# Two f tiles at a time through a two-layer network behind block attention, on one core

## The chip, the core and the metric

The kernel runs on one core of a Trainium2 chip. The engines of the core appear in the profile as PE (TensorE, matrix products, with PEld for its weight loads), DVE (VectorE), ACT (ScalarE), POOL (GpSimd) and SP (SyncE, which issues the DMAs here). The metric is the device time of one execution in microseconds (us); the number given for a kernel is the median of several runs. Times inside an execution come from one profiled execution, counted from its first instruction.

## The reference

Attention with a local window of 16 positions and, beside it, one summary key and value for each block of 32 positions; then a two-layer network with squared ReLU. B = 4 batches, H = 8 heads, S = 768 positions, D = 64; the network has 512 inputs, 2048 hidden units and 512 outputs.

```python
k_sum = k.reshape(B, H, nb, 32, D).max(axis=3)
v_sum = v.reshape(B, H, nb, 32, D).mean(axis=3)
scores_l = scale * q @ k.T          # kept where |i - j| < 16
scores_s = scale * q @ k_sum.T + log(32)
a = softmax(concat(scores_l, scores_s))
x = a @ concat(v, v_sum)            # heads side by side: 3072 tokens x 512
h = maximum(x @ w_in, 0)
out = (h * h) @ w_out
```

## The kernel before

**Tiling.** The 3072 tokens are 24 attention tiles g of 128 tokens, six (t = 0 to 5) for each batch b. Two tiles make a column block c (12 of them, CT = 256 tokens) for the network. The hidden units are 16 f tiles of 128 (NF). One f tile of one c is the unit of the network, here called a slot.

**The network.** Values are split in a high and a low part, so that each product is three matmuls: high by high, high by low, low by high. `ffn1(c, f)` (L306, matmuls at L311) is 12 matmuls of 256 columns from `xh` and `xl` into one tile `ph`. Then `squares(ph)` (L339): `relu` on ACT (L320), `high_square` on ACT (L327, gives `gh`), `square` on DVE (L332, in place in `ph`) and `low_square` on DVE (L336, gives `gl` and is the last to read `ph`). `ffn2` (L345, matmuls at L352) is 6 matmuls of 512 columns from `gh` and `gl` into the two tiles `o_ps[c]`, which gather over the 16 f tiles. `evict` (L358) copies each of the two `o_ps` tiles to `ob` on ACT (L105) and stores it; where an earlier part was parked (c = 0 and 1), it adds on DVE instead (L362).

**Buffers.** `ph` comes from a pool with three buffers (`ps_h`), `o_ps` from one with two, scores `s_ps` and attention outputs `x_ps` from one buffer each. `gh` and `gl` have three buffers each. `e_sb`, `ksum` and `vsum` exist once; `q_sb`, `k_sb`, `v_sb` and `pT` twice, by g even or odd.

**Order.** The whole program is issued in an order written out by hand: each engine takes its own instructions in that order. First comes the list START (all of attention tiles 0 to 5, the scores of tile 6, the rounding of the weights, the network of c = 0 and 1 up to f tile unit 29). Then `softmax(6, 0, 5)`, and the loop over c = 2 to 11 and f = 0 to 15, which calls `slot` (L384): `ffn1` of this f; `follow`, that is `ffn2` of two slots ago (BEHIND = 2, with both evictions after the last f of a c); the list `side`; `squares`; the list `last`. So PE has ffn1(f), ffn2(f-2), ffn1(f+1), ffn2(f-1) and so on.

**A tile's steps.** `steps(g)` (L396) spreads the attention of one tile over 11 slots; a new tile begins every 8 slots. Step 0: `place_k` (DVE, L151, only for t = 0 and 1 of a later batch, puts the block maxima into `k_sb`), at its end the scores (PE, L218) and the loads of q and k for tile g+2 (SP). Steps 1 to 3: `softmax` of 2, 3 and 3 heads, each head being one masked minimum on DVE (L231) and one exponential on ACT (L239). Steps 3 and 4: `inverse` (DVE, L248 and L249) and `norm` (POOL, L254) of each half. Steps 5 to 7: `turn`, 12 transposes on DVE (L267), four in each; step 6 also `place_v` (DVE and POOL). Step 9: `outputs` (PE, L280) and the load of v for tile g+2. Step 10: `split_x` (ACT L294, DVE L297). In tiles t = 3 and 4 of a batch the next batch's k and v are loaded pair by pair and reduced on DVE (`sum_k` L140, `sum_v` L145 and L148), two of the four pairs in each tile.

Of the kernel before, what the change touches and what calls it, by code (L numbers as in the profile page):

```python
# [12 lines left out]
F32R = mybir.dt.float32r  # L13
# [7 lines left out]
B, H, S, D = 4, 8, 768, 64  # L21
# [3 lines left out]
P = 128  # L25
NT = S // P
NPAIR = H // 2
TPC = 2
CT = TPC * P
NF = DF // P  # L30
NC4 = DM // P
SPARE = 1
BEHIND = 2
NK = 96 + NB
MASKED = -1.0e9

# [33 lines left out]
def attn_ffn_kernel(ctx: ExitStack, tc: tile.TileContext, q, k, kt, v, vt, v0, w, masks, ident, mean, out):  # L70
    nc = tc.nc
# [4 lines left out]
    work = ctx.enter_context(tc.tile_pool(name="work", bufs=2))  # L76
# [37 lines left out]
    def load_qk(g):  # L114
        load_q(g)
        load_k(g)

    def load_v(g):
        nc.sync.dma_start(out=v_sb[g % 2][0:96], in_=v[g // NT, g % NT])
# [13 lines left out]
    def load_kv(b, p):  # L133
        kv[b, p] = r = room(F32, "kv")
        nc.sync.dma_start(out=r[:, 0:S], in_=kt[b, p])
        if b:
            nc.sync.dma_start(out=r[:, S : 2 * S], in_=vt[b, p])

    def sum_k(b, p):
        nc.vector.tensor_reduce(  # L140
            out=ksum[:, p], in_=kv[b, p][:, 0:S].rearrange("a (n j) -> a n j", j=BLOCK), op=ALU.max, axis=AX.X
        )

    def sum_v(b, p):
        nc.vector.tensor_reduce(  # L145
            out=vsum[:, p, 0:NB], in_=kv[b, p][:, S : 2 * S].rearrange("a (n j) -> a n j", j=BLOCK), op=ALU.add, axis=AX.X
        )
        nc.vector.tensor_scalar_mul(vsum[:, p, 0:NB], vsum[:, p, 0:NB], 1.0 / BLOCK)  # L148

    def place_k(g):  # L150
        nc.vector.tensor_copy(out=k_sb[g % 2][:, 4], in_=ksum.unsqueeze(1).to_broadcast([P, 2, NPAIR, NB]))  # L151

    def place_v(g):
        dst = v_sb[g % 2][96:128]
        if g % 2 == 0:
            for a in range(4):
                nc.vector.transpose(
                    out=dst[:, 0, :].rearrange("a (p c) -> a p c", c=128)[:, :, a * 32 : a * 32 + 32],
                    in_=vsum[a * 32 : a * 32 + 32],
                )  # L160
        else:
            nc.gpsimd.tensor_copy(out=dst[:, 0, :], in_=v_sb[0][96:128, 0, :])
        nc.gpsimd.tensor_copy(out=dst[:, 1, :], in_=v_sb[0][96:128, 0, :])
# [46 lines left out]
    def scores(g, p0, p1):  # L210


        if g not in s_ps:
            s_ps[g] = ps_s.tile([P, 2, NPAIR, P], F32, name="s_ps")
        for p in range(p0, p1):
            for r, s in ((0, 0), (1, 1), (0, 1), (1, 0)):
                rs, ss = slice(r * 64, r * 64 + 64), slice(s * 64, s * 64 + 64)
                nc.tensor.matmul(  # L218
                    s_ps[g][ss, r, p, 0:NK], lhsT=q_sb[g % 2][rs, s, p, :], rhs=k_sb[g % 2][rs, :, s, p, :],
                    start=True, stop=True,  # L220
                )
# [19 lines left out]
    def softmax(g, h0, h1):  # L241

        for h in range(h0, h1):
            mask_max(g, h)
            exponentials(h)

    def inverse(half):
        nc.vector.tensor_scalar_add(sm[half], sm[half], 1.0e-9)  # L248
        nc.vector.reciprocal(sm[half], sm[half])  # L249
        del nmx[half]  # L250

    def norm(half, eng):
        e = e_sb[:, half * 4 : half * 4 + 4, 0:NK]
        eng.tensor_mul(out=e, in0=e, in1=sm[half].unsqueeze(2).to_broadcast([P, 4, NK]))  # L254
# [8 lines left out]
    def turn(g, n0, n1):  # L263

        blocks = [(i, j) for i in range(4) for j in ((0, 1, 3) if i % 2 == 0 else (1, 2, 3))]
        for i, j in blocks[n0:n1]:
            nc.vector.transpose(  # L267
                out=pT[g % 2][j * 32 : j * 32 + 32, :, i * 32 : i * 32 + 32],
                in_=e_sb[i * 32 : i * 32 + 32, :, j * 32 : j * 32 + 32],
            )  # L270
# [3 lines left out]
    def outputs(g):  # L274
        x_ps[g] = xp = ps_x.tile([P, NPAIR, P], F32, name="x_ps")

        for s in range(2):
            for h in range(H):
                o = (h % 2) * 64
                nc.tensor.matmul(  # L280
                    xp[o : o + 64, h // 2, s * 64 : s * 64 + 64],
                    lhsT=v_sb[g % 2][:, s, h * 64 : h * 64 + 64],
                    rhs=pT[g % 2][:, h, s * 64 : s * 64 + 64],
                    start=True, stop=True,
                )
# [13 lines left out]
    def split_x(g):  # L299
        high_x(g)  # L300
        low_x(g)
# [4 lines left out]
    def ffn1(c, f):  # L306
        ph = ps_h.tile([P, 4, P], F32, name="ph").rearrange("p a b -> p (a b)")[:, 0:CT]
        n = 0
        for cc in range(NC4):
            for w, x in ((0, xh), (1, xh), (0, xl)):  # L310
                nc.tensor.matmul(  # L311
                    ph, lhsT=w_sb[f][:, w, cc * P : (cc + 1) * P], rhs=x[c][:, cc, :], start=(n == 0), stop=(n == 3 * NC4 - 1)
                )
                n += 1
        return ph
# [7 lines left out]
        return r  # L323

    def high_square(r):
        gh = work.tile([P, CT], F32R, name="gh", tag="gh", bufs=3)
        nc.scalar.activation(gh, r, AF.Square)  # L327
        return gh

# [2 lines left out]
        nc.vector.tensor_mul(out=ph, in0=ph, in1=r)  # L332

    def low_square(ph, gh):
        gl = work.tile([P, CT], F32R, name="gl", tag="gl", bufs=3)
        nc.vector.tensor_sub(out=gl, in0=ph, in1=gh.bitcast(F32))  # L336
        return gl

    def squares(ph):  # L339
        r = relu(ph, nc.scalar)  # L340
        gh = high_square(r)
        square(ph, r)
        return gh, low_square(ph, gh)
# [30 lines left out]
    n_g = B * NT  # L374
    n_c = n_g // TPC
    behind = []
# [7 lines left out]
    def slot(c, f, side, last):  # L384


        ph = ffn1(c, f)
        if len(behind) == BEHIND:
            follow(*behind.pop(0))
        for do in side:  # L390
            do()
        behind.append((c, f, *squares(ph), f == 0, f == NF - 1))
        for do in last:
            do()

    def steps(g):  # L396


        b, t = divmod(g, NT)
        side, last = [[] for _ in range(11)], [[] for _ in range(11)]  # L400
        if b and t < 2:
            side[0].append(lambda: place_k(g))
            side[6].append(lambda: place_v(g))
        last[0].append(lambda: scores(g, 0, NPAIR))
        if g + 2 < n_g:
            last[0].append(lambda: load_qk(g + 2))
        side[1].append(lambda: softmax(g, 0, 2))
        side[2].append(lambda: softmax(g, 2, 5))
        side[3] += [lambda: inverse(0), lambda: norm(0, nc.gpsimd), lambda: softmax(g, 5, 8)]
        side[4] += [lambda: inverse(1), lambda: norm(1, nc.gpsimd)]  # L410
        for n in range(3):
            side[5 + n].append(lambda n=n: turn(g, 4 * n, 4 * n + 4))
        last[9].append(lambda: outputs(g))
        if g + 2 < n_g:
            last[9].append(lambda: load_v(g + 2))
        side[10].append(lambda: split_x(g))
        if b and t in (3, 4) and b + 1 < B:
            p = 2 * (t - 3)
            last[0].append(lambda: load_kv(b + 1, p))
            side[4] += [lambda: sum_k(b + 1, p), lambda: sum_v(b + 1, p)]  # L420
            last[4].append(lambda: load_kv(b + 1, p + 1))
            side[8] += [lambda: sum_k(b + 1, p + 1), lambda: sum_v(b + 1, p + 1)]
        return side, last


# [87 lines left out]
    with tc.manual_schedule(engines=None):  # L513
        for token in START.split():
            what, i, j, eng = re.fullmatch(r"(L:[a-z]+|F[12]|[A-Z]+)\.?(\d*)\.?(\d*)([avp]?)", token).groups()
            i, j = int(i or 0), int(j or 0)
            if what.startswith("L:"):
                load(what[2:], i)
            else:
                begin(what, i, j, engines.get(eng))  # L520
        tiles = {g: steps(g) for g in range(6, n_g)}

        def at(side, last, g, step):

            if g in tiles and 0 <= step < 11:
                side += tiles[g][0][step]
                last += tiles[g][1][step]

        load_qk(8)
        softmax(6, 0, 5)  # L530
        behind += [(*units[i][:2], *g_of[i], False, i == 31) for i in (30, 31)]
        for c in range(2, n_c):
            for f in range(NF):
                side, last = [], []
                at(side, last, 2 * c + 2, f + 3)
                at(side, last, 2 * c + 3, f - 5)
                at(side, last, 2 * c + 4, f - 13)
                slot(c, f, side, last)
        for p in behind:
            follow(*p)  # L540
# [67 lines left out]
```

## Time and profile before

| what | us |
|---|---|
| median of 3 runs | 644.5 (644.11 to 645.98) |
| the profiled execution | 646.57 |
| its span, first to last instruction | 644.8 |
| PE busy in the span | 609.8 (95%) |
| DVE busy | 403.3 (63%) |
| ACT busy | 300.4 (47%) |
| POOL busy | 108.8 (17%) |

The profiled execution's own time is 1.8 us above its span. The regular loop over slots takes from 149.7 us to the end. The busy time of PE is the time covered by its matmuls, which overlap one another: a matmul of 256 columns stands in the profile with a mean of 282 ns, but in the loop one starts about every 0.115 us. Rows of the timeline give the start, the duration, the engine, the line and the tiles written and read; in brackets stands the idle time before an instruction with what ended it.

### The profile page before, as it was taken

How to read it: one execution, taken by the hardware profiler on the slowest of the kernel's cores; microseconds unless marked ns; L12 is line 12 of the kernel's file. 1: busy time of each engine (PE TensorE's matmuls, PEld its weight loads, DVE VectorE, ACT ScalarE, POOL GpSimd, SP SyncE). 2: the span in 40 equal slices, each digit the busy share in tenths (PEclk: the TensorE clock that was granted, in tenths of full speed). 3: DMA queues.
4: the chain of work that ended last, by engine and by line, in shares of the span. 5: the costliest groups of instructions: out<-in, count | busy, mean ns of one | idle time of the engine just before them, and what ended most of it. 6: DMA issues, size and time to landing. Idle time of an engine off the chain costs nothing.

```text
span 644.8 us, 13041 instructions
## 1 busy us (share of the span) xinstructions
PE 609.8 (95%) x5052; PEld 536.3 (83%) x5052; DVE 403.3 (63%) x1223; ACT 300.4 (47%) x854; POOL 108.8 (17%) x85
## 2 busy tenths in 40 slices
PE   1678999999999999999999999999999999999997
PEld 0267988898888888898898898898888888898996
DVE  4678787656674686774774676874765665654232
ACT  2788866724335335345344344444344443443322
POOL 4465563501011011011011010010010010110000
PEclk9979999999999999999999999999999999999999
DMA  9999517004202314302102233301122020000000
GB/s 350 380 344 405 147 33 255 2 34 140 66 1 100 113 52 151 112 1 89 52 25 67 86 111 116 121 29 66 37 63 67 34 67 25 34 2 1 34 1 33
DMA packets 20429, 61.92 MB, mean 96 GB/s; under 512 B 2832, under 2 KB 2960, under 8 KB 18320
## 3 DMA queue, kind: packets, MB, share of 16 engines
q1 hardware_dynamic: 20368, 61.10, 27.6%
q8 instruction: 39, 0.64, 0.4%
q14 instruction: 22, 0.18, 0.1%
HBM read 54.80 MB, written 6.29 MB: 95 GB/s over the span
## 4 chain that ended last, share of the span: by engine, by line
PE 92%; DVE 3%; DMA 2%; ACT 1%; issue 1%; POOL 0%; SPq 0%; DVEq 0%; POOLq 0%; ACTq 0%
PE ph L311 42%; PE o_ps L352 40%; PE x_ps L280 4%; PE s_ps L218 4%; PE ph L260 1%; DMA k_sb<-in_k 1%; PE o_ps L126 1%; DMA w_raw<-in_w 1%; DVE pT L267 1%; DVE ksum L140 1%; ACT e_sb L239 0%; DVE k_sb L151 0%; ACT w_raw L189 0%; POOL e_sb L254 0%; ACT w_raw L185 0%
## 5 line engine op out<-in xcount | busy, mean ns | idle before, releaser
L311 PE MATMUL ph<-xh,w_sb 128*128 128x256 f32 x1536 | 280.4, 282 | 1.5 <-DVE gl L336 0.9
L311 PEld LDWEIGHTS ph<-xh,w_sb 128*128 128x128 f32 x1536 | 243.6, 188 | 18.8 <-issue 3.0
L352 PE MATMUL o_ps<-w_sb,gh 128*128 128x512 f32 x768 | 239.6, 393 | 0.0
L311 PE MATMUL ph<-xl,w_sb 128*128 128x256 f32 x768 | 213.9, 278 | 0.2 <-DVE xl L297 0.2
L332 DVE TENSOR_TENSOR ph<-ph,r 128x256 f32<-128x256 f32 x192 | 82.7, 431 | 125.0 <-ACT r L320 122.0
L352 PE MATMUL o_ps<-w_sb,gl 128*128 128x512 f32 x384 | 151.5, 395 | 0.0
L320 ACT ACTIVATE r<-ph 128x256 f32<-128x256 f32 x179 | 68.0, 380 | 175.3 <-PE ph L311 163.0
L352 PEld LDWEIGHTS o_ps<-w_sb,gh 128*128 128x128 f32 x768 | 131.0, 188 | 17.8 <-DVE ob L105 0.3
L311 PEld LDWEIGHTS ph<-xl,w_sb 128*128 128x128 f32 x768 | 144.9, 189 | 0.5 <-DVE xl L297 0.4
L239 ACT ACTIVATE e_sb<-e_sb,nmx 128x120 f32<-128x120 f32 x192 | 74.0, 387 | 81.8 <-DVE nmx L231 80.7
L254 POOL TENSOR_TENSOR e_sb<-e_sb,sm 128x480 f32<-128x480 f32 x42 | 41.7, 993 | 400.3 <-DVE nmx L231 360.7
L336 DVE TENSOR_TENSOR gl<-ph,gh 128x256 fp32r<-128x256 f32 x192 | 81.3, 424 | 29.0 <-ACT gh L327 7.2
L267 DVE STREAM_TRANSPOSE pT<-e_sb 32x256 f32<-32x256 f32 x216 | 94.2, 436 | 4.1 <-POOL e_sb L254 0.3
L327 ACT ACTIVATE gh<-r 128x256 fp32r<-128x256 f32 x192 | 80.2, 418 | 19.8 <-DVE r L322 7.5
L352 PEld LDWEIGHTS o_ps<-w_sb,gl 128*128 128x128 f32 x384 | 72.5, 189 | 14.8
L231 DVE CUSTOM_DVE_ANT_0 e_sb<-s_ps,mask_sb 128x120 f32<-128x120 f32 x192 | 44.0, 275 | 15.9 <-PE s_ps L218 10.6
L218 PE MATMUL s_ps<-k_sb,q_sb 64*64 64x120 f32 x768 | 27.3, 281 | 21.3 <-DVE k_sb L151 15.4
L218 PEld LDWEIGHTS s_ps<-k_sb,q_sb 64*64 64x64 f32 x768 | 21.2, 140 | 29.3 <-DVE k_sb L151 15.8
L197 POOL TENSOR_TENSOR w_raw<-w_raw 128x1024 int32<-128x1024 int32 x16 | 32.0, 2004 | 40.3 <-ACT w_raw L189 16.0
L297 DVE TENSOR_TENSOR xl<-x_ps,xh 128x512 fp32r<-128x512 f32 x24 | 16.6, 691 | 34.9 <-ACT xh L294 34.9
L239 ACT ACTIVATION_READ_ACCUMULATOR e_sb<-e_sb,nmx 128x1 f32 x192 | 36.3, 189 | 0.0
L280 PEld LDWEIGHTS x_ps<-pT,v_sb 128*64 128x64 f32 x768 | 25.6, 143 | 12.8 <-issue 9.7
(40 smaller groups left out, 290.2 us busy)
## 6 DMA issues: line engine op xcount, KB each, us to landing
w_raw<-in_w SPq DMA_DIRECT2D x16, 1024.0 KB, 11.1
k_sb<-in_k SPq DMA_DIRECT2D x24, 384.0 KB, 4.1
v_sb<-in_v SPq DMA_DIRECT2D x24, 384.0 KB, 3.9
kv<-in_kt SPq DMA_DIRECT2D x16, 384.0 KB, 5.6
q_sb<-in_q SPq DMA_DIRECT2D x24, 256.0 KB, 3.6
out<-ob SPq DMA_DIRECT2D x24, 256.0 KB, 2.1
kv<-in_vt SPq DMA_DIRECT2D x12, 384.0 KB, 6.2
vn<-in_v SPq DMA_DIRECT2D x2, 768.0 KB, 9.4
```

The lines of the kernel that those rows point to most:

```text
L218: nc.tensor.matmul(s_ps[g][ss, r, p, 0:NK], lhsT=q_sb[g % 2][rs, s, p, :], rhs=k_sb[g % 2][rs, :, s, p, :], start=True, stop=True,)
L231: nc.vector.tensor_tensor_reduce(out=e_sb[:, h, 0:NK], in0=s_ps[g][:, h % 2, h // 2, 0:NK], in1=m, scale=-scale, scalar=3.0e38, op0=ALU.ad ...
L239: nc.scalar.activation(e, e, AF.Exp, bias=nmx[half][:, i : i + 1], scale=-1.0, accum_out=sm[half][:, i : i + 1])
L254: eng.tensor_mul(out=e, in0=e, in1=sm[half].unsqueeze(2).to_broadcast([P, 4, NK]))
L267: nc.vector.transpose(out=pT[g % 2][j * 32 : j * 32 + 32, :, i * 32 : i * 32 + 32], in_=e_sb[i * 32 : i * 32 + 32, :, j * 32 : j * 32 + 32],)
L280: nc.tensor.matmul(xp[o : o + 64, h // 2, s * 64 : s * 64 + 64], lhsT=v_sb[g % 2][:, s, h * 64 : h * 64 + 64], rhs=pT[g % 2][:, h, s * 64 ...
L311: nc.tensor.matmul(ph, lhsT=w_sb[f][:, w, cc * P : (cc + 1) * P], rhs=x[c][:, cc, :], start=(n == 0), stop=(n == 3 * NC4 - 1))
L320: nc.scalar.activation(r, ph, AF.Relu)
L327: nc.scalar.activation(gh, r, AF.Square)
L332: nc.vector.tensor_mul(out=ph, in0=ph, in1=r)
L336: nc.vector.tensor_sub(out=gl, in0=ph, in1=gh.bitcast(F32))
L352: nc.tensor.matmul(o_ps[c][tt], lhsT=g_[:, ts_], rhs=w_sb[f][:, w, DM:], start=(first and n == 0), stop=(last and n == 2),)
```

## The change

`slot` now takes two f tiles: `ffn1` of f and of f+1, then `follow` for both tiles of the pair before, then for each of the two its `side` list and its `squares`, and one `last` list at the end. On PE the order is ffn1(f), ffn1(f+1), ffn2(f-2), ffn2(f-1), and then the scores or the outputs that the pair's steps hold. `gh` and `gl` get a fourth buffer; `ph` keeps three.

The steps of a tile are spread over 14 f tiles instead of 11 and laid in the pairs by even step numbers: scores at the end of the pair with step 1, softmax of 3, 3 and 2 heads at steps 2 to 4, `turn` by three transposes at steps 6 to 9, outputs at the end of the pair with step 11, `split_x` at step 12. The next batch's k and v come one pair of heads at a time in tiles t = 2 to 5, and `place_k` of the next batch's two first tiles runs at step 5 of t = 5. `place_k(7)` and six heads of tile 6 stand ahead of the loop, and tile 6 has its turns packed into two pairs.

```diff
-        gh = work.tile([P, CT], F32R, name="gh", tag="gh", bufs=3)
+        gh = work.tile([P, CT], F32R, name="gh", tag="gh", bufs=4)
...
-        gl = work.tile([P, CT], F32R, name="gl", tag="gl", bufs=3)
+        gl = work.tile([P, CT], F32R, name="gl", tag="gl", bufs=4)
...
     def slot(c, f, side, last):
-        ph = ffn1(c, f)
-        if len(behind) == BEHIND:
+        ph = [ffn1(c, f + i) for i in range(2)]
+        while behind:
             follow(*behind.pop(0))
-        for do in side:
-            do()
-        behind.append((c, f, *squares(ph), f == 0, f == NF - 1))
+        for i in range(2):
+            for do in side[i]:
+                do()
+            behind.append((c, f + i, *squares(ph[i]), f + i == 0, f + i == NF - 1))
         for do in last:
             do()
...
-        side, last = [[] for _ in range(11)], [[] for _ in range(11)]
+        side, last = [[] for _ in range(14)], [[] for _ in range(14)]
+        last[1].append(lambda: scores(g, 0, NPAIR))
+        if g + 2 < n_g:
+            last[1].append(lambda: load_qk(g + 2))
         if b and t < 2:
-            side[0].append(lambda: place_k(g))
-            side[6].append(lambda: place_v(g))
-        last[0].append(lambda: scores(g, 0, NPAIR))
+            side[7].append(lambda: place_v(g))
+        side[2].append(lambda: softmax(g, 0, 3))
+        side[3].append(lambda: softmax(g, 3, 6))
+        side[4] += [lambda: inverse(0), lambda: norm(0, nc.gpsimd), lambda: softmax(g, 6, 8)]
+        side[5] += [lambda: inverse(1), lambda: norm(1, nc.gpsimd)]
+        for n in range(4):
+            side[6 + n].append(lambda n=n: turn(g, 3 * n, 3 * n + 3))
+        last[11].append(lambda: outputs(g))
         if g + 2 < n_g:
...
+            last[11].append(lambda: load_v(g + 2))
+        side[12].append(lambda: split_x(g))
+        if b and t >= 2 and b + 1 < B:
+            last[1].append(lambda: load_kv(b + 1, t - 2))
+            side[4].append(lambda: sum_k(b + 1, t - 2))
+            side[5].append(lambda: sum_v(b + 1, t - 2))
+        if t == NT - 1 and b + 1 < B:
+            side[5] += [lambda: place_k(g + 1), lambda: place_k(g + 2)]
...
-            if g in tiles and 0 <= step < 11:
-                side += tiles[g][0][step]
-                last += tiles[g][1][step]
-
+            for i in range(2):
+                if g in tiles and 0 <= step + i < 14:
+                    side[i] += tiles[g][0][step + i]
+                    last += tiles[g][1][step + i]
+
+        place_k(7)
         load_qk(8)
-        softmax(6, 0, 5)
+        softmax(6, 0, 6)
+
+        side = tiles[6][0]
+        side[6:10] = [side[6], side[7] + side[8] + side[9], [], []]
...
-            for f in range(NF):
-                side, last = [], []
-                at(side, last, 2 * c + 2, f + 3)
-                at(side, last, 2 * c + 3, f - 5)
-                at(side, last, 2 * c + 4, f - 13)
+            for f in range(0, NF, 2):
+                side, last = [[], []], []
+                at(side, last, 2 * c + 2, f + (4 if c == 2 else 6))
+                at(side, last, 2 * c + 3, f - 2)
+                at(side, last, 2 * c + 4, f - 10)
                 slot(c, f, side, last)
```

More of the change, by code (lines that the diff above doesn't have):

```diff
@@ L32 @@
 SPARE = 1
-BEHIND = 2
 NK = 96 + NB
@@ L399, in steps @@
         b, t = divmod(g, NT)
-        side, last = [[] for _ in range(11)], [[] for _ in range(11)]
+        side, last = [[] for _ in range(14)], [[] for _ in range(14)]
+        last[1].append(lambda: scores(g, 0, NPAIR))
+        if g + 2 < n_g:
+            last[1].append(lambda: load_qk(g + 2))
         if b and t < 2:
-            side[0].append(lambda: place_k(g))
-            side[6].append(lambda: place_v(g))
-        last[0].append(lambda: scores(g, 0, NPAIR))
-        if g + 2 < n_g:
[L406 to L422, printed above, removed]
+            side[7].append(lambda: place_v(g))
[6 more added lines that the diff above has]
+        last[11].append(lambda: outputs(g))
+        if g + 2 < n_g:
+            last[11].append(lambda: load_v(g + 2))
[6 more added lines that the diff above has]
+            side[5] += [lambda: place_k(g + 1), lambda: place_k(g + 2)]
         return side, last
```

## The prediction

> **What bounds the kernel now.** The page comes first: TensorE (PE) is busy for nearly the whole span.
>
> ```profile
> span 644.8 us, 13041 instructions
> ...
> PE 609.8 (95%) x5052; PEld 536.3 (83%) x5052; DVE 403.3 (63%) x1223; ACT 300.4 (47%) x854; POOL 108.8 (17%) x85
> ```
>
> A busy PE may still be a PE in small waits, so I next asked for a middle stretch, and for everything that PE waited for from 149.7 us on, where the regular loop begins.
>
> ```profile
> 300.00:400.00 100.00, 98.80 (x838) 87.71 (x838) 64.92 (x213) 42.64 (x137) 9.75 (x12) 1.00 0.23 77
> ```
>
> ```profile
> PE s_ps L218 <- issue: 2.0, 2, 1.2
> PE s_ps L218 <- DVE k_sb L151: 0.9, 1, 0.9
> PE ph L311 <- ACT xh L294: 0.7, 1, 0.7
> PE ph L311 <- DVE xl L297: 0.2, 1, 0.2
> ```
>
> In the first row the columns after the length are busy time of PE, PEld, DVE, ACT and POOL, then the granted clock. In the loop of 495 us PE waits 3.8 us. So whatever the change does for the other engines, it can win only what PE still loses; and every delay that it makes on DVE or ACT costs nothing until it reaches PE. PE's own rows, timeline of one f tile (ffn2 at L352, ffn1 at L311, start first):
>
> ```profile
> 402.29 0.62 PE L352 MATMUL o_ps<-w_sb,gh 128*128 128x512 f32 x2
> ...
> 403.67 0.40 PE L311 MATMUL ph<-xh,w_sb 128*128 128x256 f32 x2
> ...
> 404.71 0.39 PE L311 MATMUL ph<-xh,w_sb 128*128 128x256 f32 x2
> ...
> 405.05 0.62 PE L352 MATMUL o_ps<-w_sb,gh 128*128 128x512 f32 x2
> ```
>
> A row of ffn2 takes 1.38 us (402.29 to 403.67), one of ffn1 1.38 us (403.67 to 405.05). Within ffn1 the last three matmuls take 0.34 (404.71 to 405.05), but the nine before them 1.04 and not 1.02: about 0.02 to 0.03 us is lost after the switch from ffn2.
>
> **The change, part by part.**
>
> *Pairs on PE.* The same matmuls run in the order ffn1, ffn1, ffn2, ffn2. The second ffn1 row has no switch before it: it should take 4 x 0.34 = 1.36 instead of 1.38. The loop has 160 f tiles, so 80 second rows; at 0.025 us that is **2.0 us gained**. No row shows ffn1 directly behind ffn1, so the bounds are 0 and 80 x 0.03 = 2.4.
>
> *place_k.* Today it is issued in the slot whose scores need it. One of three such places (two DVE rows, then PE's):
>
> ```profile
> 316.02 0.42 DVE L336 TENSOR_TENSOR gl<-ph,gh 128x256 fp32r<-128x256 f32 x1
> 316.36 0.25 DVE L151 COPY k_sb<-ksum 128x192 f32<-128x192 f32 x1
> ```
>
> ```profile
> 316.71 1.05 PE L218 MATMUL s_ps<-k_sb,q_sb 64*64 64x120 f32 x32 [1.20 <-issue]
> ```
>
> PE's wait is entered as "issue", but the scores start right after place_k, which stood behind a square. The two "issue" waits and the k_sb wait of the list above are these: 2.0 + 0.9 = 2.9 us. The change issues place_k for both next tiles at step 5 of a block's last tile, four steps before the first of those scores, and for tile 7 ahead of the loop, two pairs before its scores. Its 0.25 us each then lie on DVE behind a ready tile. **2.9 us gained**; bounds 0 and 2.9, and nothing suggests that it stays.
>
> *The wait that is added.* ffn1 has three ph buffers, so ffn1 of f+3 must wait until the GL (low_square, L336) of f has read ph. Today three slots lie between them. In a pair only 5.5 us lie between the end of ffn1(f) and the start of ffn1(f+3), f being the first of a pair: ffn1(f+1), two ffn2 rows, ffn1(f+2). This wait exists on the chip; it is seen once in the start (DVE's row, then PE's):
>
> ```profile
> 106.28 0.42 DVE L336 TENSOR_TENSOR gl<-ph,gh 128x256 fp32r<-128x256 f32 x1 [2.97 <-ACT gh L327]
> ```
>
> ```profile
> 106.76 0.51 PE L311 MATMUL ph<-xh,w_sb 128*128 128x256 f32 x2 [0.86 <-DVE gl L336]
> ...
> 108.15 0.28 PE L311 MATMUL ph<-xl,w_sb 128*128 128x256 f32 x1
> ```
>
> GL ends at 106.70 and PE starts 0.06 later. That row ran 106.76 to 108.26 (its last matmul at 0.11), 1.50 us: 0.14 more than a row that flows.
>
> Whether GL(f) is late depends on what stands ahead of it on ACT and DVE. At a new c, follow() now runs ffn2 of c-1's f=14 and f=15 **and its two evictions** in pair 0, ahead of squares(0). ACT takes its queue in order. What that does, from today's boundary, ACT first and then DVE:
>
> ```profile
> 403.18 1.27 ACT L105 COPY ob<-o_ps 128x512 f32<-128x512 f32 x2 [1.26 <-PE o_ps L352]
> 404.35 0.39 ACT L320 ACTIVATE r<-ph 128x256 f32<-128x256 f32 x1
> 404.77 0.42 ACT L327 ACTIVATE gh<-r 128x256 fp32r<-128x256 f32 x1
> ```
>
> ```profile
> 402.41 0.16 DVE L248 TENSOR_SCALAR sm<-sm 128x4 f32<-128x4 f32 x1
> 402.61 0.18 DVE L249 RECIPROCAL sm<-sm 128x4 f32<-128x4 f32 x1
> 402.70 0.92 DVE L140 TENSOR_REDUCE ksum<-kv 128x24 f32<-128x768 f32 x1
> 403.54 0.94 DVE L145 TENSOR_REDUCE vsum<-kv 128x24 f32<-128x768 f32 x1
> 404.52 0.18 DVE L148 TENSOR_SCALAR vsum<-vsum 128x24 f32<-128x24 f32 x1
> 404.77 0.43 DVE L332 TENSOR_TENSOR ph<-ph,r 128x256 f32<-128x256 f32 x1
> 405.34 0.42 DVE L336 TENSOR_TENSOR gl<-ph,gh 128x256 fp32r<-128x256 f32 x1
> ```
>
> Let R be the start of the last ffn2 row of c-1 (402.29). The evictions hold ACT until its relu starts at R + 2.06 (404.35); the square follows at R + 2.48, GL ends at R + 3.47 (405.76). Today the held tile is f=1, whose buffer is wanted three slots later. After the change the held tile is f=0, although its ffn1 ended 2.7 us before R; in pair 0 ACT has nothing else, and DVE only three transposes, before it. PE after R: the ffn2 row 1.38, ffn1(2) 1.38, so ffn1(3) is due at R + 2.76 and can start at R + 3.47 + 0.06 = R + 3.53. PE waits 0.77, plus 0.14 for starting anew: 0.91 us. It comes at c = 3 to 11, nine times: **8.2 us lost**. Tile 1's own squares come behind but have over 3 us more to go.
>
> By the Trainium skill (Perfetto Trace Analysis, Optimization Strategy), a gap that repeats on the engine that should be full can mean too little room for the next tile; the wait at 106.76 is of that kind, and by this rule the price above stays as long as ph has three buffers.
>
> *The first pair (c=2).* There the evictions are additions on DVE, and inverse, norm and two heads of tile 6 stand between them and squares(0). PE's last ffn2 row of c=1 today, then DVE, then a head and its exponential (ACT):
>
> ```profile
> 154.53 0.63 PE L352 MATMUL o_ps<-w_sb,gh 128*128 128x512 f32 x2
> ```
>
> ```profile
> 155.43 1.38 DVE L362 TENSOR_TENSOR ob<-o_ps,ob 128x512 f32<-128x512 f32 x2
> 156.73 0.16 DVE L248 TENSOR_SCALAR sm<-sm 128x4 f32<-128x4 f32 x1
> ```
>
> ```profile
> 152.58 0.25 DVE L231 CUSTOM_DVE_ANT_0 e_sb<-s_ps,mask_sb 128x120 f32<-128x120 f32 x1
> ```
>
> ```profile
> 152.87 0.40 ACT L239 ACTIVATE e_sb<-e_sb,nmx 128x120 f32<-128x120 f32 x1 [0.25 <-DVE nmx L231]
> ```
>
> The row starts at the same place after the change (two ffn1 and one ffn2 row from 149.7 on, in another order): R = 154.53. The inverse starts at 156.73, the head 0.29 later (as 402.41 to 402.70) at 157.02, its exponential 0.29 later at 157.31, two of them at 0.39 each to 158.09; relu to square 0.42, square to GL 0.57, GL 0.42: 159.50, PE at 159.56. Due at R + 2.76 = 157.29: 2.27 + 0.14 = **2.4 us lost**. What follows (nine transposes and place_v in one half of a pair) ends close to its due time; bounds 0 and 0.8, I take 0.2, since only one square looks late.
>
> *The other pairs.* The longest list on DVE ahead of a pair's first squares is at step 4: split_x, the inverse, two heads, sum_k. It begins about 0.7 us after the pair does (ACT's half of split_x), and takes 0.69 + 0.29 + 2 x 0.2 + 0.92 = 2.3, so GL ends near 0.7 + 2.3 + 0.57 + 0.42 = 4.0 us after the pair's start and is wanted at 1.38 + 5.5 = 6.9. Softmax in threes holds ACT for 3 x 0.39 from the pair's start, about until ffn1 ends. So nothing there reaches PE; cover of nearly 3 us would have to go first, at 0.9 us a place. One term of that list has a page row:
>
> ```profile
> L297 DVE TENSOR_TENSOR xl<-x_ps,xh 128x512 fp32r<-128x512 f32 x24 | 16.6, 691 | 34.9 <-ACT xh L294 34.9
> ```
>
> *Loads.* On SP, load_kv still stands behind load_qk, which waits for the scores; it is now one pair of kv loads at each of four tiles instead of two at each of two.
>
> ```profile
> kv<-in_kt SPq DMA_DIRECT2D x16, 384.0 KB, 5.6
> ```
>
> Issued an estimated 1 us after the scores (behind two loads of some 0.4 us on SP), it lands at 6.6; sum_k is reached a pair later, at 6.8 (5.5 and the outputs) + 1.4 = 8.2. It costs nothing; were it 2 us late, GL would still be in time. norm on POOL and load_v keep their distance. gh and gl with four buffers add no instruction.
>
> **Sum.** Lost 8.2 + 2.4 + 0.2 = 10.8, gained 2.0 + 2.9 = 4.9: **+5.9 us**. The profiled execution's span of 644.8 becomes 650.7, its own time of 646.57 becomes 652.5. The median of the runs shown, 644.5, lies 2.1 below that execution; I put the sum on the median: **650.4 us**.
>
> **Rivals.** (1) *The ph wait does not bind*: were GL(0) over at R + 2.70 instead of R + 3.47, the 10.8 would vanish and 644.5 - 4.9 = **639.6** is left. For it: the wait never binds in today's loop, and DVE and ACT are idle for a third and more. Against it: the order on ACT is plain in the rows, and 0.77 us is missing each time. 0.13. (2) *It nearly cancels*: restart free, second rows at their best, the first pair covered: 9 x 0.6 - 5.3, about **644.6**. 0.08, with the case that the order on PE makes no difference at all. (3) *Further waits*: a kv load so late that the step 4 squares reach PE too, over 3 us beyond the reckoning; eight tiles at 0.9 more, **657.6**. 0.05. (4) *The clock falls in the new gaps*: the third of the page's 40 slices has clock 7, the lowest; if the 2.3 us gap brought such a slice (644.8 / 40 = 16.1 us, a third slower), 16.1 x 0.3 = 4.8 more, **655.2**. Against it: the row of 300 to 400 us, with the 1.20 us wait in it, has clock 1.00. 0.02. The clock by slices:
>
> ```profile
> PEclk9979999999999999999999999999999999999999
> ```
>
> The Trainium skill (TensorE: Matmul & The Clock Gate, Part 1) has the clock halved after an idle window of some 3.4 us; by that rule none of these gaps is long enough.
>
> **How the numbers follow.** Forecast 0.72: the terms' bounds (restart 0 to 0.14, first pair 1 to 3, pairs 0 to 2.4) give 645 to 654. Of the rest, 0.13 lies below. A measurement tells about 0.3% (1.9 us) from no change: faster 0.13, within 0.08, slower 0.79. The range 645.0 to 654.5 leaves out (1), (3), (4) and part of (2).
>
> **What would show it.** Right: the list of PE's waits has "ph L311 <- DVE gl", about ten times, 0.8 each, one near 2.3 at about 157 us, each in the second ffn1 row of the second pair of a c; the scores' waits are gone; second ffn1 rows take 1.36. Wrong: no such entry, or ACT's relu of f=0 ahead of the copies to ob (then rival 1), or waits on k_sb and kv (then 3).

## The result and the profile after

The changed kernel is slower: 651.62 us (649.32 to 652.63, 4 runs) beside 644.45 us for the kernel before; the ratio is 1.0102, with a 95% interval of 1.0070 to 1.0133. The forecast was 650.4.

The page of the changed kernel shows as much PE work as before in a longer span, and a new releaser behind ffn1 (now L310; GL, low_square, is now L335, ffn2 L351):

```profile
span 650.2 us, 13010 instructions
...
PE 610.5 (94%) x5052; PEld 535.7 (82%) x5052; DVE 402.5 (62%) x1223; ACT 294.2 (45%) x854; POOL 108.8 (17%) x85
...
L310 PE MATMUL ph<-xh,w_sb 128*128 128x256 f32 x1536 | 278.3, 283 | 8.1 <-DVE gl L335 7.4
```

All that PE waited for from 146 us on (in total, times, longest):

```profile
PE ph L310 <- DVE gl L335: 7.4, 10, 2.0
PE ph L310 <- ACT xh L293: 0.7, 1, 0.7
PE ph L310 <- DVE xl L296: 0.2, 1, 0.2
PE o_ps L351 <- DVE gl L335: 0.2, 1, 0.2
```

The waits of the scores are gone, and ten waits on GL have come. One of the nine regular ones, the boundary at 405 us: ACT, then DVE, then PE.

```profile
405.00 1.27 ACT L104 COPY ob<-o_ps 128x512 f32<-128x512 f32 x2 [6.36 <-PE o_ps L351]
406.17 0.39 ACT L319 ACTIVATE r<-ph 128x256 f32<-128x256 f32 x1
406.59 0.42 ACT L326 ACTIVATE gh<-r 128x256 fp32r<-128x256 f32 x1
```

```profile
406.59 0.43 DVE L331 TENSOR_TENSOR ph<-ph,r 128x256 f32<-128x256 f32 x1 [4.54 <-ACT r L319]
407.15 0.42 DVE L335 TENSOR_TENSOR gl<-ph,gh 128x256 fp32r<-128x256 f32 x1
```

```profile
406.76 0.28 PE L310 MATMUL ph<-xl,w_sb 128*128 128x256 f32 x1
407.63 0.50 PE L310 MATMUL ph<-xh,w_sb 128*128 128x256 f32 x2 [0.60 <-DVE gl L335]
...
409.12 0.62 PE L351 MATMUL o_ps<-w_sb,gh 128*128 128x512 f32 x2
```

ACT is idle for 6.36 us, because the next thing in its queue is a copy whose source PE has not finished; the relu of f=0, long ready, stands behind it. DVE then waits for the relu, GL ends at 407.57, and PE, which has nothing else in its order, starts ffn1(3) 0.06 later. Counted by starts, as the prediction counts, the wait is 0.76 us: after the matmul at 406.76 the next was due 0.11 later, at 406.87. The brackets show 0.60, since they count from the end of the matmul before (the expectations below write 0.68 for the same wait). The row that follows takes 1.49 (407.63 to 409.12) instead of 1.36.

Executions differ in how fast the part before the loop runs (the loop begins at 149.72 in the first profile of the kernel before, at 147.11 in that of the changed one), so from here on **the loop** is compared: from the first ffn1 of c=2 to the start of the last matmul. It took 491.06 us before (149.72 to 640.78) and 499.11 after (147.11 to 646.22), 8.0 us more; the spans alone (644.8 and 650.2) show 5.4. The blocks that matter, as differences of the starts of the first ffn1 of each c (c=11: to the start of the last matmul), and the loops of all kernels, in us (e6 apart):

| kernel | c=2 | c=3 | c=5 | c=8 | c=11 | loop |
|---|---|---|---|---|---|---|
| before | 50.97 | 49.05 | 50.31 | 49.97 | 46.68 | 491.06 |
| changed | 53.45 | 49.73 | 50.21 | 50.21 | 48.01 | 499.11 |
| e1 | 49.44 | 48.84 | 48.84 | 48.84 | 46.46 | 485.45 |
| e2 | 49.44 | 49.73 | 50.23 | 50.21 | 47.44 | 494.57 |
| e3 | 53.35 | 48.84 | 48.84 | 48.84 | 46.46 | 489.36 |
| e4 | 49.66 | 49.05 | 49.05 | 49.05 | 46.68 | 487.58 |
| e5 | 51.90 | 48.85 | 50.15 | 50.15 | 46.46 | 490.95 |
| e7 | 50.36 | 49.05 | 49.05 | 49.05 | 46.68 | 488.29 |
| changed again (e8) | 53.34 | 49.73 | 50.21 | 50.21 | 47.35 | 498.31 |

### The profile page after: what moved, and what is told of

Same layout as the page of the kernel before. It is cut to its first block, busy times and chain, and to the rows that moved or that the text cites. A ratio compares the mean times of both kernels' runs of the same rounds, so it can differ in the third digit from the quotient of the medians.

```text
span 650.2 us, 13010 instructions
## 1 busy us (share of the span) xinstructions
PE 610.5 (94%) x5052; PEld 535.7 (82%) x5052; DVE 402.5 (62%) x1223; ACT 294.2 (45%) x854; POOL 108.8 (17%) x85
## 4 chain that ended last, share of the span: by engine, by line
PE 91%; DVE 4%; DMA 2%; ACT 1%; issue 1%; POOL 0%; SPq 0%; DVEq 0%; POOLq 0%; ACTq 0%
PE ph L310 42%; PE o_ps L351 40%; PE x_ps L279 4%; PE s_ps L217 3%; PE ph L259 1%; DMA k_sb<-in_k 1%; PE o_ps L125 1%; DMA w_raw<-in_w 1%; DVE gl L335 1%; ACT e_sb L238 1%; DVE ksum L139 1%; DVE pT L266 0%; DVE v_sb L156 0%; DVE k_sb L150 0%; ACT w_raw L184 0%
## 5 line engine op out<-in xcount | busy, mean ns | idle before, releaser
L310 PE MATMUL ph<-xh,w_sb 128*128 128x256 f32 x1536 | 278.3, 283 | 8.1 <-DVE gl L335 7.4
L310 PEld LDWEIGHTS ph<-xh,w_sb 128*128 128x128 f32 x1536 | 238.9, 190 | 20.1 <-DVE gl L335 9.4
L351 PE MATMUL o_ps<-w_sb,gh 128*128 128x512 f32 x768 | 239.1, 393 | 0.0
L310 PE MATMUL ph<-xl,w_sb 128*128 128x256 f32 x768 | 214.6, 279 | 0.2 <-DVE xl L296 0.2
L351 PEld LDWEIGHTS o_ps<-w_sb,gh 128*128 128x128 f32 x768 | 136.9, 189 | 24.1 <-ACT r L319 0.2
L351 PE MATMUL o_ps<-w_sb,gl 128*128 128x512 f32 x384 | 151.7, 395 | 0.4 <-DVE gl L335 0.2
L310 PEld LDWEIGHTS ph<-xl,w_sb 128*128 128x128 f32 x768 | 145.8, 190 | 0.5 <-DVE xl L296 0.4
L335 DVE TENSOR_TENSOR gl<-ph,gh 128x256 fp32r<-128x256 f32 x192 | 81.4, 424 | 26.0 <-ACT gh L326 5.2
L351 PEld LDWEIGHTS o_ps<-w_sb,gl 128*128 128x128 f32 x384 | 72.3, 188 | 16.0 <-DVE gl L335 1.2
L230 DVE CUSTOM_DVE_ANT_0 e_sb<-s_ps,mask_sb 128x120 f32<-128x120 f32 x192 | 43.9, 275 | 16.1 <-PE s_ps L217 10.8
L104 ACT COPY ob<-o_ps 128x512 f32<-128x512 f32 x22 | 12.9, 587 | 62.9 <-PE o_ps L351 61.9
```

Of the source, the lines that this page charges most:

```text
L230: nc.vector.tensor_tensor_reduce(out=e_sb[:, h, 0:NK], in0=s_ps[g][:, h % 2, h // 2, 0:NK], in1=m, scale=-scale, scalar=3.0e38, op0=ALU.ad ...
L310: nc.tensor.matmul(ph, lhsT=w_sb[f][:, w, cc * P : (cc + 1) * P], rhs=x[c][:, cc, :], start=(n == 0), stop=(n == 3 * NC4 - 1))
L351: nc.tensor.matmul(o_ps[c][tt], lhsT=g_[:, ts_], rhs=w_sb[f][:, w, DM:], start=(first and n == 0), stop=(last and n == 2),)
```

## The experiments

### e1 to e3: the evictions behind the squares

```diff
-    def follow(c, f, gh, gl, first, last):
+    late = []
+
+    def follow(c, f, gh, gl, first, last, wait=False):
         ffn2(c, f, gh, gl, first, last)
         if last:
             for tt in range(TPC):
-                evict(c, f, tt, nc.scalar)
+                if wait:
+                    late.append((c, f, tt, nc.scalar))
+                else:
+                    evict(c, f, tt, nc.scalar)
...
         while behind:
-            follow(*behind.pop(0))
+            follow(*behind.pop(0), True)
         for i in range(2):
...
             behind.append((c, f + i, *squares(ph[i]), f + i == 0, f + i == NF - 1))
+        while late:
+            evict(*late.pop(0))
```

This is e1; e2 has c == 2 in the place of True, e3 has c > 2.

> The changed kernel with the two evictions of a column block issued after both squares of the pair, instead of ahead of them. Loop = first ffn1 of c=2 to the last matmul: 491.1 us before, 499.1 after. Theory (ffn1(3) waits for the ph buffer that GL(0) holds, GL(0) being late because ACT, or DVE at c=2, does the evictions first): all ten waits of PE on GL go; nine at 0.92 = 8.3, the one at c=2 2.1 and the half clock behind it 1.6, and some 1.6 of slower rows and late GL behind the waits: loop near 485.6, time near 638 to 639, faster than before by about 5.4 us (place_k waits 3.2, second rows 2.1). Rival 1 (rows in pairs cost PE time by themselves): loop stays above 497. Rival 2 (the wait moves: the next ffn2 then waits for o_ps that is evicted too late): the list of PE's waits names ob instead of gl, loop about 497.

> As e1, but the evictions are late in the first pair of the loop (c=2) alone. Theory: the 2.0 us wait there goes, and with it the 3.4 us at half clock that begins 0.6 us after it: 2.1 + 1.6 = 3.7 off the loop, 495.4. Rival (the half clock comes by itself and not from this wait): 2.1 off, 497.0, and a stretch of clock 0.5 stays near 157 us. The nine waits of c=3 to 11 stay at 0.68 each in the starts of neighbouring matmuls.

> As e1, but the evictions are late for c=3 to 11 alone. Theory: 9 x 0.92 = 8.3 off, and with the waits the slower rows behind them at c=11 (0.6) and the two places where ffn2 waited for gl (1.0): loop 499.1 - 9.9 = 489.2. The wait at c=2 of 2.0 us and the half clock behind it stay. If only the nine waits count: 490.8. Rival 1 (pairs cost by themselves): above 497.

e1 took 639.14 us beside 644.39 of the kernel before, a ratio of 0.9920 (0.9906 to 0.9933): **moving two instructions makes the change a gain**, and e1 is faster than both kernels. Its loop of 485.45 is the 485.6 expected. PE's waits from 145 us on are these:

```profile
PE ph L310 <- ACT xh L293: 0.7, 1, 0.7
PE ph L310 <- DVE xl L296: 0.2, 1, 0.2
```

At a boundary ACT now has the squares done 1.2 us before the copies can begin, and the copies start as soon after their matmuls as ever:

```profile
394.19 0.39 ACT L319 ACTIVATE r<-ph 128x256 f32<-128x256 f32 x1 [0.53 <-PE ph L310]
394.61 0.42 ACT L326 ACTIVATE gh<-r 128x256 fp32r<-128x256 f32 x1
396.25 1.27 ACT L104 COPY ob<-o_ps 128x512 f32<-128x512 f32 x2 [1.23 <-PE o_ps L351]
```

No wait on ob has come, so the second rival falls, and rows in pairs cost nothing by themselves, so does the first. e3 (643.54 us, one run) takes 9.75 off the loop, where 9.9 was expected from nine waits, the late gl at c=5 and c=8, and c=11. e2 (646.76 us, one run) takes 4.5 off; 4.0 of it lie in c=2, and 0.6 in c=11, which its edit does not touch (see e8). In e2 neither the wait of 2.0 us nor the half clock is left; the changed kernel and e2, the columns after the length being busy PE, PEld, DVE, ACT, POOL and then the clock:

```profile
157.43:160.85 3.42, 3.42 (x14) 3.04 (x13) 2.83 (x8) 1.09 (x3) 0.81 (x1) 0.50 0.02 5
```

```profile
157.00:160.50 3.50, 3.50 (x50) 2.85 (x49) 3.37 (x9) 0.00 (x0) 0.61 (x1) 1.00 0.02 8
```

PE is "busy" in the whole of both stretches, but starts 14 matmuls in the one and 50, many of them small, in the other: busy time hides the halved clock, the clock column shows it.

### e4: place_k alone

```diff
-            side[0].append(lambda: place_k(g))
...
+        if t == NT - 1 and b + 1 < B:
+            side[4] += [lambda: place_k(g + 1), lambda: place_k(g + 2)]
...
+        place_k(7)
         load_qk(8)
         softmax(6, 0, 5)
```

> The kernel before with place_k alone moved: for the next batch's two first tiles at step 4 of a batch's last tile, for tile 7 ahead of the loop. Theory: the three waits of the scores (0.99, 1.27, 0.91) go: loop 491.1 - 3.2 = 487.9, time 641.3. Rival: the wait is passed on to the next slot's square or softmax and the loop stays within 0.5 of 491.1.

It took 640.87 us, a ratio of 0.9950 (0.9936 to 0.9963) to the kernel before; the loop lost 3.5 us, all of it in c=2, c=5 and c=8, and PE's list names no scores any more. Nothing was passed on. Against e4, e1 has what the pairs bring: 48.84 instead of 49.05 in each full block, 0.21 for eight second rows, 0.026 us each, 2.1 us in the loop. A second row in e1 takes 1.36:

```profile
404.79 0.39 PE L310 MATMUL ph<-xh,w_sb 128*128 128x256 f32 x2
...
406.15 0.62 PE L351 MATMUL o_ps<-w_sb,gh 128*128 128x512 f32 x2
```

### e5: more room for ph instead of another order

```diff
...
-        ph = [ffn1(c, f + i) for i in range(2)]
+        both = bank()
+        ph = [ffn1(c, f + i, both[:, i * CT : (i + 1) * CT]) for i in range(2)]
```

bank() is the tile that ffn1 took for itself, of which it used half.

> The changed kernel, evictions where they were, but the two ph of a pair share one buffer (each half of it), so that three buffers hold six ph and ffn1 of f+3 no longer waits for GL of f. Theory (it is the ph buffer that carries the late GL to PE): the ten ph waits go although GL(0) is as late as before; what is left is at c=2, where gl(0) comes some 0.4 us after ffn2(2,0) wants it, perhaps with slower rows behind: loop 485.5 to 486.5, time near 639.5. Rival (the late squares reach PE by another way, as gl for ffn2 or through o_ps): loop stays above 490 and PE's waits name gl before ffn2 or ob. Second rival (sharing a buffer makes relu wait for the second ffn1 row and so costs): relu starts 1.36 later, seen on ACT alone.

It took 644.59 us beside 644.03, a ratio of 1.0002 (0.9992 to 1.0012). The ph waits are gone, as expected: c=3, 4 and 7 take 48.85. But the loop is 490.95 instead of 486, because of the rival: where place_v lies between the two squares of a pair, the lateness reaches PE one step further on, as gl for ffn2. PE's list of e5, then DVE and PE at c=5:

```profile
PE o_ps L354 <- DVE gl L338: 3.7, 3, 1.6
```

```profile
304.61 0.42 DVE L338 TENSOR_TENSOR gl<-ph,gh 128x256 fp32r<-128x256 f32 x1
305.07 1.26 DVE L156 STREAM_TRANSPOSE v_sb<-vsum 32x128 f32<-32x128 f32 x4
306.36 1.33 DVE L266 STREAM_TRANSPOSE pT<-e_sb 32x256 f32<-32x256 f32 x3
307.73 0.43 DVE L334 TENSOR_TENSOR ph<-ph,r 128x256 f32<-128x256 f32 x1
308.27 0.42 DVE L338 TENSOR_TENSOR gl<-ph,gh 128x256 fp32r<-128x256 f32 x1
```

```profile
308.75 0.50 PE L354 MATMUL o_ps<-w_sb,gl 128*128 128x512 f32 x1 [1.03 <-DVE gl L338]
```

The three waits are at c=2, 5 and 8. So the ph buffer is how the delay reaches PE in the ordinary blocks, but the cause is the late square, and of the two edits only the order cures all blocks. The second rival's sign came too, on ACT alone: in the pair at 323 us the second ffn1 row begins at 324.59 and the relu of f=0 only at 326.15, after that row; in e1 (394 us) the relu begins 0.20 after the start of the second row. The relu of f=1 then waits 0.58 us for the GL of f=0. (c=6 takes 49.23 because one GL starts 0.4 us late; the trace names no releaser for it.)

### e6: the suspected delay in doses

```diff
+MORE = {2: 1, 3: 2, 4: 3, 5: 4, 6: 2, 7: 3, 8: 1, 9: 5, 10: 3}
...
             copy(eng, ob, o_ps[c][tt])
+            for _ in range(MORE.get(c, 0) * tt):
+                copy(eng, ob, o_ps[c][tt])
```

> The changed kernel with further copies of the second o_ps tile to its ob behind the evictions on ACT: for c=3 to 11 in order 1, 2, 3, 4, 2, 3, 1, 5, 3 of them (c=2 as it was); the output is unchanged. Theory: each copy delays GL(0), and so PE, by one step of ACT of about 0.5 us (the second eviction of the boundary at 403 us began 0.69 after the first, bound by PE; the relu 0.48 after the second): the waits of 0.68 in the changed kernel become 1.2, 1.7, 2.2, 2.7, 1.7, 2.2, 1.2, 3.2, 2.2. Rival (something else holds PE): the waits do not grow in these steps. For the clock: if a wait of about 2 us is what halves it, stretches of 0.5 of 3.4 us follow the waits of 2.2 us and over (c=5, 6, 8, 10, 11), and perhaps those of 1.7; if it takes an idle time of 3.4 us, as the page TensorE: Matmul & The Clock Gate of the Trainium skill has it (Part 1), none of them.

The key is the evicted block, one below the c in which the copies run. 671.95 us, one run. Waits with one, two, three and five copies, from PE's timeline:

```profile
208.37 0.50 PE L311 MATMUL ph<-xh,w_sb 128*128 128x256 f32 x2 [1.22 <-DVE gl L336]
...
259.34 0.69 PE L311 MATMUL ph<-xh,w_sb 128*128 128x256 f32 x2 [1.84 <-DVE gl L336]
...
312.52 0.50 PE L311 MATMUL ph<-xh,w_sb 128*128 128x256 f32 x2 [2.46 <-DVE gl L336]
...
573.00 0.50 PE L311 MATMUL ph<-xh,w_sb 128*128 128x256 f32 x2 [3.69 <-DVE gl L336]
```

From 0.60 without a copy they grow by 0.62 for each, up to 3.69: what ACT does ahead of squares(0) goes one to one into PE's time. (The step was expected at 0.5; with the further copies ACT's row of copies is 1.89 instead of 1.27 long, so 0.62 is one copy's own length.) The clock fell after four of the nine waits, and after that of c=2; the last section has the pattern.

### e7: the control

```diff
-            for tt in range(TPC):
-                evict(c, f, tt, nc.scalar)
+            late.extend((c, f, tt, nc.scalar) for tt in range(TPC))
...
         behind.append((c, f, *squares(ph), f == 0, f == NF - 1))
+        while late:
+            evict(*late.pop(0))
```

> The kernel before with the evictions issued after the squares of their slot, as e1 has them: a control. Theory (the order on ACT matters only where a ph buffer is wanted 5.5 us after its ffn1): today's squares of f=1 come 2 us late and nobody waits for them, so the loop stays at 491.1 (within 0.3). Rival (late evictions save time in any order of PE): loop near 483 to 487.

The control did not stay: 641.59 us (one run, beside 643.51), loop 488.29, 2.8 us off, all at c=2, 5 and 8, the places of the place_k waits. My reading of the kernel before was incomplete. Its DVE at c=5, before the wait at 315 us that the prediction shows:

```profile
303.25 0.18 DVE L249 RECIPROCAL sm<-sm 128x4 f32<-128x4 f32 x1
305.41 0.43 DVE L332 TENSOR_TENSOR ph<-ph,r 128x256 f32<-128x256 f32 x1 [1.99 <-ACT r L320]
```

From that idle 1.99 us on (the relu stood behind the evictions) DVE hardly pauses until place_k at 316.36: place_v, twelve transposes and the squares of four tiles leave it no room to catch up. In e7 the square of f=1 starts 4.8 us after its block does instead of 6.6, and PE's list keeps one short wait of the scores:

```profile
PE s_ps L218 <- DVE k_sb L151: 0.4, 1, 0.4
```

So somebody did wait for the late squares of the kernel before, four slots later. Early place_k (e4) and late evictions (e7) are two cures of one delay. Their gains cannot add up: after e4 PE's list has no wait left that e7 could remove.

### e8: once more

> The changed kernel once more, unaltered, for what may differ between executions. What follows from the program must come back: ten waits on GL, nine of them 0.68 longer than neighbouring starts, the one at c=2 2.0 us with 3.4 us of half clock behind it, late gl at c=5 and c=8. Open: in the first profile of this kernel the rows of c=11 behind its wait took 2.83 us a pair of ffn1 instead of 2.75 (0.6 us in all), in e2 they did not. If it is chance, c=11 takes either 47.4 or 48.0 us; if it belongs to this kernel, 48.0 again. Loop 498.5 to 499.1.

650.73 us (one run); the ten waits, 7.4 us in all, the half clock behind the one of c=2 and the two late gl came back. c=11 took 47.35, not 48.01: the slow rows of the first profile were of that execution. With them out, the changed loop is 7.25 us longer than before, which is the difference of the medians (7.2).

## Why the prediction was right, and where its terms were not

**Pairs on PE (2.0 gained):** right, 2.1 by e1 against e4.

**place_k (2.9 gained):** right in size, 3.5 by e4, which counts PE's restart too. The reason was half of it: place_k stood behind a square, but that square was late because of the evictions, as e7 shows. The prediction saw the evictions' delay as harmless in the kernel before ("the wait never binds in today's loop"); the ph wait indeed never binds there, but the delay behind it reached PE all the same, by way of place_k.

**The ph wait (0.91 at nine places, 8.2 lost):** right. A plain block takes 49.73 with the wait and 48.84 without it (e3), 0.89 a place and 8.0 in all; the row at 407.63 has it as 0.76 of waiting, for 0.77, and 0.13 for starting anew, for 0.14. e1 and e3 remove it by order alone, e5 by room alone, e6 makes it grow. What did not hold is the remark that this price stays as long as ph has three buffers: e1 has three and does not pay it.

**The first pair (2.4 lost):** the wait was nearly as worked out (2.0 us in the list, 2.2 by starts, for 2.27), the price was not: 4.0 by the c=2 column of the changed kernel and e2. The step that failed is rival 4. It got 0.02 because the stretch of 300 to 400 us, with a wait of 1.20 us, has clock 1.00; the rule of the Trainium skill that stands beside it (TensorE: Matmul & The Clock Gate, Part 1) would have left the clock alone too. But 3.4 us at clock 0.50 follow the wait of 2.0 us, worth 1.7; the rival itself had put 4.8 on a longer stretch of 16.1 us.

**Late squares after the boundary (0.2 lost, put at c=2):** mis-sized and misplaced. At c=2 no ffn2 waited in the first profile. At c=5 and c=8 "over 3 us more to go" was spent by place_v, which lies ahead of the second square of pair 0. The changed kernel at c=5, DVE and then PE:

```profile
307.68 1.26 DVE L156 STREAM_TRANSPOSE v_sb<-vsum 32x128 f32<-32x128 f32 x4
308.98 1.34 DVE L266 STREAM_TRANSPOSE pT<-e_sb 32x256 f32<-32x256 f32 x3
310.35 0.43 DVE L331 TENSOR_TENSOR ph<-ph,r 128x256 f32<-128x256 f32 x1
310.91 0.42 DVE L335 TENSOR_TENSOR gl<-ph,gh 128x256 fp32r<-128x256 f32 x1
```

```profile
310.55 0.62 PE L351 MATMUL o_ps<-w_sb,gh 128*128 128x512 f32 x2
311.39 0.50 PE L351 MATMUL o_ps<-w_sb,gl 128*128 128x512 f32 x1 [0.22 <-DVE gl L335]
```

Two matmuls flow in 0.46; here 0.84 passes to the third, and the next is slow too: about 0.5 at each of the two places, 1.0 in all.

**Other pairs, loads:** right; no wait on kv, k_sb or softmax stands in the changed kernel's list.

**The sum:** 8.0 + 4.0 + 1.0 lost and 3.5 + 2.1 gained is 7.4 in the loop, where 7.25 (e8) and, with 0.6 of slow rows, 8.05 were measured and 5.9 predicted. The missing 1.5 is the half clock and place_v, less what place_k gave more. The number came out nearer than its terms: the first pair and the late squares were put too low by 2.4 together, and the other three errors, 0.9 together, go the other way. The first pair (bounds 1 to 3), the late squares (0 to 0.8) and place_k (0 to 2.9) all ended beyond their bounds, so part of the agreement is luck.

## What to carry to other kernels

When the order on one engine is stretched (here ffn1 in pairs), every buffer's distance from its use to its reuse changes: work it out for the shortest case, and then ask what stands ahead of the releasing instruction in its own queue. An instruction that must wait for a late producer should be issued behind those that are ready; here two copies moved by a few lines turned 1.0102 into 0.9920. A delay on an engine that is idle a third of the time may still reach the bound engine several steps later, so a wait is traced back past its releaser until an idle gap is found.

## What the runs showed of the hardware

**The clock halves after a window that is somewhat more than half idle, not only after a whole idle one.** The half-clock stretches of e6 behind its waits begin at 157.1, 259.5, 365.3, 573.5 and 624.7 us (the first behind the wait of c=2); their distances are whole multiples of 3.413 (30, 31, 61 and 15 times), so the windows form a fixed grid. Three windows of that grid and the one behind each:

```profile
256.07:259.49 3.42, 1.58 (x14) 1.39 (x13) 1.03 (x3) 3.21 (x8) 0.00 (x0) 1.00 0.38 148
259.49:262.90 3.41, 3.41 (x15) 3.22 (x16) 3.16 (x8) 1.29 (x4) 0.00 (x0) 0.50 0.02 8
```

```profile
310.69:314.10 3.41, 1.58 (x13) 1.58 (x14) 2.39 (x7) 2.54 (x7) 0.19 (x1) 1.00 0.20 77
314.10:317.51 3.41, 3.19 (x20) 2.05 (x22) 3.16 (x8) 0.80 (x2) 0.42 (x1) 1.00 0.01 2
```

```profile
621.30:624.71 3.41, 1.25 (x11) 1.06 (x10) 0.61 (x2) 3.25 (x8) 0.00 (x0) 1.00 0.26 99
624.71:628.13 3.42, 3.12 (x13) 3.06 (x14) 1.77 (x5) 1.23 (x4) 0.00 (x0) 0.50 0.14 55
```

PE is busy for 1.58 and 1.25 us in the first and the third, and the next window has clock 0.50. In the second it is busy for 1.58 too, and the clock keeps 1.00. In e6 a wait of 1.84 us that falls into one window halves the clock, and a wait of 2.46 that the grid cuts in two (310.06 to 312.52) does not. In the ten traces of this case, from 30 us on, the half clock follows every full-clock window of the grid in which PE is idle for 2.00 us or more (31 of them), and none with 1.83 us or less. Two lie between and contradict each other: 1.84 us (the first above) halves it, and 1.90 us at the end of e5 does not:

```profile
637.72:641.14 3.42, 1.51 (x7) 0.92 (x5) 0.00 (x0) 1.17 (x2) 0.00 (x0) 1.00 0.32 120
641.14:642.86 1.72, 0.00 (x0) 0.00 (x0) 0.00 (x0) 0.00 (x0) 0.00 (x0) 1.00 0.17 67
```

So the point lies here at about 1.8 to 2.0 us of idle time in a window, and busy time as the profile shows it does not fix it more closely. The page TensorE: Matmul & The Clock Gate of the Trainium skill (Part 1) has the grid of some 3.4 us right, but gives an idle window as the condition; these runs show that somewhat over half a window is enough.

**Rows behind a wait can stay slow.** In the first profile of the changed kernel, after the wait at c=11, a pair of ffn1 rows took 2.83 us instead of 2.75 to the end; in e2 and e8, which have the same wait, it did not. What decides it stays open.
